# One-core attention and expert kernel: slot table and row order made by one-hot products instead of index scatters, one raw-key buffer, two squares at step 4

## The chip, the cores and the metric

The kernel runs on one core of a Trainium2 chip. A core has five engines with a queue of instructions each: TensorE (PE, matmuls and transposes), VectorE (DVE), ScalarE (ACT), GpSimd (POOL) and SyncE (SP, which here issues most DMAs). Transfers run on 16 DMA engines. An engine takes its instructions in order; one that waits holds back all behind it. The metric is the device time of one execution, in microseconds; the median of the runs counts.

## What is computed

Attention with pooled queries, then routed experts, then a gated product with two more weight matrices:

```python
B, H, S, D = q.shape                                    # 4, 8, 1152, 64
q_pool = q.reshape(B, H, S // 2, 2, D).mean(axis=3)     # 576 rows
scores = np.matmul(q_pool, k.transpose(0, 1, 3, 2)) / np.sqrt(D)
attn = exp(scores - max); attn /= attn.sum(-1) + 1e-9
x = np.matmul(attn, v)                                  # -> (2304, 512)

do_compute = x @ w_skip > 0                             # rows that go to an expert
logits = x[do_compute] @ w_gate                         # 8 experts
e_idx, gate_w = argmax(logits), softmax(logits)[e_idx]
for e in range(8):                                      # w1 (512,1024), w2 (1024,512) of expert e
    y[e_idx == e] = gate_w * (relu(x @ w1[e]) @ w2[e])
out[do_compute] = x + y ; the other rows stay x

a, b = out @ m1, out @ m2                               # (512,1024) each
result = ((a * b) @ w3) @ w_out                         # (1024,1024), (1024,512)
```

m1, m2, w3 and w_out come as 64-bit floats and are brought to 32 bits in the kernel.

## The kernel before

**Attention.** 16 pairs of heads p, four for each of four batches; a pair has nine steps, which a loop runs through as i = 0..143 (p, l = divmod(i, 9)) and a few more to drain. Step i issues, in this order: on PE the nine transposes (L289) of step i−2's probabilities, whose three parts ACT, DVE and ACT copy out of PSUM (L308); on ACT the exponentials (L278) of step i−1; on PE the products with v (L325); on PE the score matmuls (L255) of step i, and on DVE their maximum (L266). POOL prepares keys (L208, L209) and queries (L214 to L222) of later pairs in `prep`, SP moves them. The raw keys `kr` have two buffers. Between the transposes and copies, and at the end of a step, `side` lets two generators go on by a piece:

- `conv_ops` brings the 64-bit weights to 32 bits, chunk by chunk: a load to `ch`, the square L82 (on POOL, 128x512), the scaling and bit operations L96 to L104 (on DVE), a store. The squares of the first two chunks stand together in one piece.
- `route_ops` routes one batch of 576 rows (five groups j of 128 rows) once its attention is done: expert and skip score, one-hot rows, ranks by a triangular matmul (L391, L393; the banks are the `VB` pair), then for each row a place `si` in the table of slots (expert e begins at e·2304) and a place `sp` in the order of all rows. Ten indirect DMAs on POOL (`put`, L417) scatter the row numbers `idt` by these to the DRAM tables `tab` and `perm`. Then five groups of rows x are turned by PE (L448), scaled by DVE (L451) into one of four `xr` buffers, given their gate weight (L454) and stored by SP to `x_d` (L456). The batches 0, 1 and 2 are routed inside the loop, from steps 44, 80 and 116 on.

**Transition.** The last batch is routed after the loop. Between its pieces `fill` issues pieces of `wprime`, the product of w3 and w_out (matmuls L513, b<-CC,WS; blocks RW of w3 are loaded by ACT, L558, split into a high and a low half by ACT, L554, and DVE or POOL, L555 and L556). `emit_meta` computes on DVE the table of expert tiles (first slot and expert of each); only with it does SP issue the loads of W1 (L608) and read the 128 row numbers of a tile from `tab` (`ld_idx`, L587). `ORD` is read from `perm` (L823). POOL gathers rows of `x_d` by them (L592 for tiles, L568 for the final groups), and W1 and W2 are split into halves by ACT, DVE and POOL.

**After it.** 11 expert tiles of 128 rows, then six groups of 384 rows with m1, m2 and the product of wprime, scattered to the output by `ORD`.

The code is issued in the order in which it is written; the engines run it by semaphores.

Of the kernel before, what the change touches and what calls it, by code (L numbers as in the profile page):

```python
# [19 lines left out]
NTT = 5  # L20
# [8 lines left out]
NJ = NTILE + 1  # L29
CW = 512  # L30
# [13 lines left out]
def body(ctx, tc, q, k, v, w9, w1, w2, m1, m2, w3t, wo, cst, mcst, ids, out, dbg=None):  # L44
# [17 lines left out]
    padt = const.tile([128, 145], I32, name="padt")  # L62

    x_d = dram.tile([N, XW], F32, name="x_d")
    tab = dram.tile([SLOTS + 128, 1], I32, name="tab")
    perm = dram.tile([N, 1], I32, name="perm")
# [7 lines left out]
    def conv_ops(erl):  # L74
# [12 lines left out]
        ms = [sq(nxt[0]), sq(nxt[1])]  # L87
        for n, (name, c) in enumerate(conv_q):
# [31 lines left out]
    if True:  # L120
# [7 lines left out]
        KH = [pl[i].tile([128, S], F32R, name=f"kh{i}") for i in range(2)]  # L128
        KL = mid.tile([128, S], F32R, name="kl")
# [9 lines left out]
        def load(p):  # L139
# [4 lines left out]
            rawk[p] = erl.tile([128, S], F32, tag="kr", name="kr", bufs=2)  # L144
# [192 lines left out]
        def route_ops(b, hook=None):  # L337
# [69 lines left out]
            si = keep.tile([128, NTT, 1], I32, tag="si", name="si")  # L407
            DVE.tensor_scalar(si, po, float(PADID), None, op0=ALU.add)
# [3 lines left out]
            sp_ = keep.tile([128, NTT, 1], I32, tag="sp", name="sp")  # L412
            DVE.tensor_tensor(sp_, tp_, pb[:, :, NE:NE + 1], op=ALU.add)
            scat = {id(tab): [], id(perm): []}

            def put(t, ix, j, top):
                m = POOL.indirect_dma_start(  # L417
                    out=t[:, :], out_offset=bass.IndirectOffsetOnAxis(ap=ix[:, j, :], axis=0),
                    in_=idt[:, b, j:j + 1], in_offset=None, bounds_check=top, oob_is_err=False).ins
                for e in scat[id(t)]:  # L420
                    tc.declare_no_dep(m, e, reason="other slots")
                scat[id(t)].append(m)

            if hook:
                for j in range(NTT):
                    put(tab, si, j, SLOTS - 1)
                for j in range(NTT):
                    put(perm, sp_, j, N - 1)
            else:
                for j in range(NTT):  # L430
                    put(tab, si, j, SLOTS - 1)
                    put(perm, sp_, j, N - 1)
                    yield "C"
# [543 lines left out]
```

## Time and profile before

| | us |
|---|---|
| median of 3 runs (1098.1 to 1102.2) | 1099.67 |
| profiled execution, its own time | 1107.73 |
| its span in the trace | 1105.6 |
| PE busy in the span | 1031.4 (93%) |
| DVE busy | 583.6 (53%) |
| ACT busy | 482.3 (44%) |
| POOL busy | 393.7 (36%) |
| attention and routes of batches 0 to 2 | until about 560 |
| last route and wprime | about 560 to 632 |
| expert tiles | 632 to 780 |
| final groups | 780 to 1106 |

A share of busy time is a mean over stretches with different limits. The clock in the windows is the one that PE was granted, as a share of 2.4 GHz. Idle time is put down to the event that came last before the engine went on.

### The profile page before, as it was taken

The numbers are of one execution on the slowest core, as the hardware profiler recorded it, in microseconds if no ns is written. First come the engines' busy times: TensorE is split into PE (matmuls) and PEld (weight loads), VectorE is DVE, ScalarE is ACT, GpSimd is POOL, SyncE is SP. The second block draws the span as 40 slices with busy tenths as digits, with TensorE's granted clock in tenths as the row PEclk, the third lists the DMA queues.
The fourth block names the chain that finished last, engine by engine and source line by source line (L and its number), as shares of the span: only waits on it lengthen the run. The fifth ranks groups of instructions, "written<-read, shape, count | busy, mean of one in ns | idle before, by whom it ended". The sixth has DMA issues, their size and how long they took to land. (4 is left out here: it accounts for less than half of the span.)

```text
span 1105.6 us, 16864 instructions
## 1 busy us (share of the span) xinstructions
PE 1031.4 (93%) x6060; PEld 834.8 (76%) x6060; DVE 583.6 (53%) x883; ACT 482.3 (44%) x903; POOL 393.7 (36%) x411
## 2 busy tenths in 40 slices
PE   5799999999999899899998699998899999999995
PEld 4577776777767677676776488786799898989894
DVE  6588888788876788775633322437531221213120
ACT  4466665666655566565521322434432221212120
POOL 4643524563544435250824623439301010110101
PEclk9899999999999999999999699999899999999998
DMA  9776787587874878527518841506101010100000
GB/s 265 193 229 195 225 234 219 117 192 218 250 223 89 186 212 251 151 66 150 163 39 125 265 168 40 188 24 240 34 10 48 14 44 20 39 33 26 29 1 31
DMA packets 73003, 144.92 MB, mean 131 GB/s; under 512 B 16576, under 2 KB 26304, under 8 KB 72898
## 3 DMA queue, kind: packets, MB, share of 16 engines
q1 hardware_dynamic: 63698, 127.79, 41.7%
q0 software_dynamic: 6080, 14.26, 4.0%
q10 hardware_dynamic: 3120, 1.57, 0.9%
q8 instruction: 53, 0.87, 0.4%
q14 instruction: 52, 0.43, 0.1%
HBM read 86.23 MB, written 22.96 MB: 99 GB/s over the span
## 5 line engine op out<-in xcount | busy, mean ns | idle before, releaser
L266 DVE TENSOR_REDUCE sm<-s 128x1 f32<-128x1152 f32 x144 | 195.3, 1356 | 117.5 <-PE s L255 91.5
L255 PE MATMUL s<-k,q 128*128 128x384 f32 x864 | 204.9, 364 | 29.4 <-DVE pt L308 17.3
L255 PEld LDWEIGHTS s<-k,q 128*128 128x128 f32 x864 | 147.2, 192 | 98.1 <-issue 46.9
L308 ACT COPY pt<-s 128x384 f32<-128x384 f32 x288 | 137.6, 479 | 179.9 <-PE s L289 173.9
L278 ACT ACTIVATE p<-s,sm 128x1152 f32<-128x1152 f32 x144 | 176.3, 1224 | 16.6 <-DVE sm L266 16.1
L325 PE MATMUL vb<-pt,vr 128*64 128x256 f32 (+1 forms) x1152 | 170.7, 418 | 4.3 <-DVE xr L451 2.5
L289 PE MATMUL s<-cs,p 128*128 128x128 f32 x1296 | 169.7, 277 | 4.0 <-ACT p L278 3.6
L289 PEld LDWEIGHTS s<-cs,p 128*128 128x128 f32 x1296 | 151.2, 143 | 14.8 <-ACT p L278 7.5
L887 DVE TENSOR_TENSOR ar<-b,ar 128x384 f32<-128x384 f32 x48 | 26.7, 557 | 189.7 <-PE b L883 189.7
L902 POOL DMA_INDIRECT out_dram<-ar,ord x18 | 17.9, 994 | 271.0 <-ACT ar L901 266.3
L325 PEld LDWEIGHTS vb<-pt,vr 128*64 128x64 f32 x1152 | 70.2, 136 | 56.7 <-issue 22.5
L308 DVE COPY pt<-s 128x384 f32<-128x384 f32 x144 | 78.8, 547 | 2.7 <-PE s L289 1.8
L209 POOL TENSOR_TENSOR kl<-kr,kh 128x384 fp32r<-128x384 f32 x45 | 47.5, 1056 | 77.2 <-DMA k<-kl 66.6
L888 ACT CAST CVh<-ar 128x384 fp32r<-128x384 f32 x48 | 24.6, 513 | 107.7 <-DVE ar L887 107.7
L82 POOL TENSOR_TENSOR cm<-ch 128x512 f32<-128x512 f32 x40 | 42.1, 1057 | 76.1 <-DVE ca L104 47.1
L513 PE MATMUL b<-W1h,CVh 128*128 128x512 f32 x176 | 60.1, 402 | 0.7 <-issue 0.5
L513 PE MATMUL b<-W2h,CVh 128*128 128x512 f32 x176 | 60.7, 404 | 0.2
L513 PE MATMUL b<-WPh,CVh 128*128 128x512 f32 x144 | 57.4, 399 | 0.0
L513 PE MATMUL b<-WPl,CVh 128*128 128x512 f32 x144 | 56.9, 395 | 0.0
L513 PE MATMUL b<-WPh,CVl 128*128 128x512 f32 x144 | 56.8, 394 | 0.0
L901 ACT COPY ar<-b 128x512 f32<-128x512 f32 x18 | 10.6, 587 | 86.2 <-PE b L513 86.2
L208 POOL TENSOR_SCALAR kh<-kr 128x384 fp32r<-128x384 f32 x45 | 26.3, 584 | 57.9 <-PE s L255 52.1
(194 smaller groups left out, 1799.0 us busy)
## 6 DMA issues: line engine op xcount, KB each, us to landing
R<-in_w_dram SPq DMA_DIRECT2D x16, 1024.0 KB, 8.8
vr<-in_v_dram SPq DMA_DIRECT2D x16, 576.0 KB, 4.9
kr<-in_k_dram SPq DMA_DIRECT2D x15, 576.0 KB, 5.3
qr<-in_q_dram SPq DMA_DIRECT2D x15, 576.0 KB
k<-kh SPq DMA_DIRECT2D x30, 288.0 KB, 5.7
k<-kl SPq DMA_DIRECT2D x30, 288.0 KB, 15.3
q<-qnl SPq DMA_DIRECT2D x60, 144.0 KB, 4.2
ch<-in_w3t_dram SPq DMA_DIRECT2D x16, 512.0 KB, 4.8
```

The lines of the kernel that those rows point to most:

```text
L82: POOL.tensor_tensor(m, hf, hf, op=ALU.mult)
L208: POOL.tensor_scalar(KH[i][:, cc], rawk[p][:, cc], 1.0, 0.0, op0=ALU.mult, op1=ALU.add)
L209: POOL.tensor_tensor(KL[:, cc], rawk[p][:, cc], f(KH[i][:, cc]), op=ALU.subtract)
L255: m = PE.matmul(sp[:, c, 0:384], lhsT=lt, rhs=kk[:, 384 * c:384 * c + 384], start=(n == 0), stop=(n == len(seq) - 1))
L266: DVE.tensor_reduce(sm, sp[:, :, 0:384], axis=AX.XY, op=ALU.max, negate=True)
L278: ACT.activation(pt, sp[:, :, 0:384], AF.Exp, bias=sm, scale=1.0, accum_out=SM[b][:, hp, c:c + 1])
L289: m = PE.transpose(tp[:, u * 128:u * 128 + 128], src[:, kt * 128:kt * 128 + 128], ident)
L308: m = (DVE.tensor_copy(o, i_) if eng is DVE else ACT.copy(o, i_)).ins
L325: PE.matmul(acc[64 * h:64 * h + 64, 0:n], lhsT=vr[:, h, kt, :], rhs=pt[:, kt, h, :], start=(kt == 0), stop=(kt == KT - 1))
L513: PE.matmul(o, lhsT=lh[a], rhs=rh[b_], start=(first and n == 0), stop=(last and n == len(order) - 1))
L887: DVE.tensor_tensor(cv, pb[:, 0:GT], av, op=ALU.mult)
L888: ACT.copy(CV[0][:, c], cv)
```

## The change

1. *Index tables without scatters.* `tab`, `perm` and their first filling are gone. A table `slots` (128 x 164: 144 + 2 columns for the slots, 18 for the order) stays in SBUF. For each group j four tensor_scalars make one-hot matrices: place & 127 against a row of 0..127 (twice, 128x128), place >> 7 against 0..145 and 0..17, multiplied by row number + 1. They stand in one of two buffers `ob` and are made on POOL for the batches 0 to 2; in the last route on DVE, in R3's memory, for all five groups. Two matmuls of 146 and 18 columns (L452, or L443 for all groups together) give the group's part of the table, which DVE adds to `slots`. The five groups of a batch each take a "P" piece of `route_ops`: steps 55, 57, 58, 59 and 62 for batch 0 and 36 and 72 later. The five groups of x move by one such place. The last route has one "P" more, so that two more pieces of `wprime` come ahead of what follows it.
2. *Reading.* `ld_idx` copies a column of `slots` from SBUF to SBUF; `ORD` is a view of the last 18 columns, with no load.
3. *Constants.* At i = 2 a matmul and four DVE operations make the row 0..145.
4. *Raw keys.* `kr` has one buffer; the second head of pair 0 is loaded into `kl`.
5. *Squares.* The two first squares have a piece for themselves, called at i = 4; the conversion then goes on from step 6 instead of 8. The steps of the route that only let the conversion go on ("C") are gone.

```diff
-            rawk[p] = erl.tile([128, S], F32, tag="kr", name="kr", bufs=2)
+            rawk[p] = erl.tile([128, S], F32, tag="kr", name="kr", bufs=1)
...
-                rawk[0, h] = erl.tile([128, S], F32, tag="kr", name="kr", bufs=2)
+                rawk[0, h] = f(KL) if h else erl.tile([128, S], F32, tag="kr", name="kr", bufs=1)
...
-            def put(t, ix, j, top):
-                m = POOL.indirect_dma_start(
-                    out=t[:, :], out_offset=bass.IndirectOffsetOnAxis(ap=ix[:, j, :], axis=0),
-                    in_=idt[:, b, j:j + 1], in_offset=None, bounds_check=top, oob_is_err=False).ins
...
-                    put(tab, si, j, SLOTS - 1)
-                    put(perm, sp_, j, N - 1)
-                    yield "C"
...
+            DVE.tensor_scalar(hl[:, 0], si, 127, None, op0=ALU.bitwise_and)
+            DVE.tensor_scalar(hl[:, 1], si, 7, None, op0=ALU.logical_shift_right)
+            hf_ = keep.tile([128, 2, 2, NTT], F32, tag="hf", name="hf", bufs=1)
+            DVE.tensor_copy(hf_, hl)
+            E = DVE if hook else POOL
...
+            def build(j):
+                t = ob[j] = obs[j % len(obs)]
+                for u in range(2):
+                    E.tensor_scalar(t[:, 128 * u:128 * u + 128], iota[:, 0:128], hf_[:, 0, u, j:j + 1], None,
+                                    op0=ALU.is_equal)
+                for u, c0, n in ((0, 256, NSL), (1, 256 + NSL, NCNT)):
+                    E.tensor_scalar(t[:, c0:c0 + n], iota[:, 0:n], hf_[:, 1, u, j:j + 1], idf[:, b, j:j + 1],
+                                    op0=ALU.is_equal, op1=ALU.mult)
...
+            for j in range(len(obs)):
+                build(j)
+            if len(obs) == NTT:
+                yield "P"
+                tp = tbank()
+                for u, c0, n in parts:
+                    for j in range(NTT):
+                        t = ob[j]
+                        PE.matmul(tp[:, c0:c0 + n], lhsT=t[:, 128 * u:128 * u + 128], rhs=t[:, 256 + c0:256 + c0 + n],
+                                  start=(j == 0), stop=(j == NTT - 1))
+                DVE.tensor_tensor(slots, tp[:, 0:NSL + NCNT], slots, op=ALU.add)
             else:
                 for j in range(NTT):
+                    yield "P"
+                    tp = tbank()
+                    t = ob.pop(j)
+                    for u, c0, n in parts:
+                        PE.matmul(tp[:, c0:c0 + n], lhsT=t[:, 128 * u:128 * u + 128], rhs=t[:, 256 + c0:256 + c0 + n],
+                                  start=True, stop=True)
+                    DVE.tensor_tensor(slots, tp[:, 0:NSL + NCNT], slots, op=ALU.add)
+                    if j + len(obs) < NTT:
+                        build(j + len(obs))
             if hook:
-                hook()
+                fr_ = hook[1]
+                DVE.tensor_scalar(fr_, slots, 0.0, float(PADID + 1), op0=ALU.is_equal, op1=ALU.mult)
+                DVE.scalar_tensor_tensor(TAB, slots, -1.0, fr_, op0=ALU.add, op1=ALU.add)
+                hook[0]()
...
-            SP.dma_start(IDX[j % 5], tab[bass.ds(st, 128), :])
+            SP.dma_start(IDX[j % 5], TAB[:, bass.ds(st, 1)])
...
-                        if g == 1 and i > 7:
-                            side("DC")
+                        if g == 1 and i > 5:
+                            side("D")
...
+                if i == 4:
+                    next(conv)
...
-            SP.dma_start(ORD, perm.rearrange("(c p) o -> p (c o)", p=128))
```

How the instructions stand on their engines at three places follows; the line numbers are those of each kernel, so that L82, L208, L214 and L222 of before are L83, L211, L217 and L225 of after.

POOL in the steps 3 to 7, before (`bd` and `qnl` are pair 1's queries, `kh` and `kl` pair 2's keys, `qsum` its queries, `cm` the squares):

```order
L222 TENSOR_SCALAR bd_110<-qnl 64x64 x2
L208 TENSOR_SCALAR kh_111<-kr 128x384
L209 TENSOR_TENSOR kl<-kr,kh_111 128x384
L208 TENSOR_SCALAR kh_111<-kr 128x384
L209 TENSOR_TENSOR kl<-kr,kh_111 128x384
L208 TENSOR_SCALAR kh_111<-kr 128x384
L209 TENSOR_TENSOR kl<-kr,kh_111 128x384
L214 TENSOR_TENSOR qsum<-qr 128x576
L215 TENSOR_SCALAR qsum<-qsum 128x576
L82 TENSOR_TENSOR cm<-ch 128x512 x2
```

The same place after:

```order
L225 TENSOR_SCALAR bd_110<-qnl 64x64 x2
L83 TENSOR_TENSOR cm<-ch 128x512 x2
L211 TENSOR_SCALAR kh_111<-kr 128x384
L212 TENSOR_TENSOR kl<-kr,kh_111 128x384
L211 TENSOR_SCALAR kh_111<-kr 128x384
L212 TENSOR_TENSOR kl<-kr,kh_111 128x384
L211 TENSOR_SCALAR kh_111<-kr 128x384
L212 TENSOR_TENSOR kl<-kr,kh_111 128x384
L83 TENSOR_TENSOR cm<-ch 128x512
L217 TENSOR_TENSOR qsum<-qr 128x576
```

The first two squares moved from behind pair 2's keys to ahead of them, and the third to directly behind them.

PE at the end of step 55 and the beginning of step 56, before (`s` the scores' bank, `vb` the bank of the products with v):

```order
L255 MATMUL s<-k_116,q_101 128x384
L255 MATMUL s<-k_116,q_102 128x384
L255 MATMUL s<-k_116,q_101 128x384
L255 MATMUL s<-k_116,q_102 128x384
L289 MATMUL s<-cs,p 128x128 x9
L325 MATMUL vb_91<-pt_2021,vr 64x256 x4
```

And after (`ob` is a buffer of one-hot matrices):

```order
L258 MATMUL s<-k_118,q_101 128x384
L258 MATMUL s<-k_118,q_102 128x384
L258 MATMUL s<-k_118,q_101 128x384
L258 MATMUL s<-k_118,q_102 128x384
L452 MATMUL vb_91<-ob_113 128x146
L452 MATMUL vb_91<-ob_113 128x18
L292 MATMUL s<-cs,p 128x128 x9
L328 MATMUL vb_91<-pt_2034,vr 64x256 x4
```

The first group's two matmuls stand between the scores of step 55 and the transposes of step 56; POOL builds `ob` where its first scatters stood.

SP in the last route, before (`R` is a half of W1, `ix` a tile's 128 row numbers):

```order
L608 DMA R_5577<-in_w_dram 128x4x512
L456 DMA x_d<-xr_83 128x516
L456 DMA x_d<-xr_84 128x516
L456 DMA x_d<-xr_85 128x516
L456 DMA x_d<-xr_86 128x516
L456 DMA x_d<-xr_83 64x516
L823 DMA ord<-perm 128x18x1
L586 TENSOR_LOAD meta
L586 ISA x2
L587 REGISTER_ALU
L587 DMA ix_120<-tab 128x1
```

And after:

```order
L634 DMA R_5607<-in_w_dram 128x4x512
L482 DMA x_d<-xr_83 128x516
L482 DMA x_d<-xr_84 128x516
L482 DMA x_d<-xr_85 128x516
L482 DMA x_d<-xr_86 128x516
L482 DMA x_d<-xr_83 64x516
L612 TENSOR_LOAD meta
L612 ISA x2
L613 ISA
L613 DMA ix_122<-slots 128x1
```

The load of ORD is gone, and the index column comes from `slots`; the order of W1, the stores and the columns is the same.

## Rows read from the trace of the kernel before

**Rows 1.** Windows: us; busy (count) PE, PEld, DVE, ACT, POOL; clock, DMA share, GB/s.

```profile
60.00:560.00 500.00, 480.13 (x3276) 355.63 (x3275) 385.92 (x544) 310.08 (x586) 227.19 (x244) 1.00 0.69 186
...
604.00:632.00 28.00, 13.45 (x41) 10.19 (x40) 6.43 (x11) 7.18 (x13) 14.77 (x16) 0.70 0.79 233
```

**Rows 2.** PE's waits on DVE's copy: us in total, times, longest.

```profile
PE s L255 <- DVE pt L308: 17.3, 11, 6.3
```

**Rows 3.** PE's timeline, begin of steps 8, 9 and 11: start, us, operation.

```profile
35.91 1.15 PE L289 MATMUL s<-cs,p 128*128 128x128 f32 x9
...
39.39 1.15 PE L289 MATMUL s<-cs,p 128*128 128x128 f32 x9
...
54.58 1.15 PE L289 MATMUL s<-cs,p 128*128 128x128 f32 x9
```

**Rows 4.** Timelines of POOL and DVE around the first squares.

```profile
30.86 0.54 POOL L222 TENSOR_SCALAR bd<-qnl 64x64 fp32r<-64x64 f32 x2
...
43.40 2.03 POOL L82 TENSOR_TENSOR cm<-ch 128x512 f32<-128x512 f32 x2
...
30.76 0.55 DVE L308 COPY pt<-s 128x384 f32<-128x384 f32 x1
...
44.47 1.51 DVE L96 SCALAR_TENSOR_TENSOR cm<-cm,ch 128x512 f32<-128x512 f32 x1 [6.48 <-POOL cm L82]
```

**Rows 5.** PE's timeline: steps 58 and 60, then 94, 96 and 99.

```profile
220.85 1.15 PE L289 MATMUL s<-cs,p 128*128 128x128 f32 x9
...
227.88 1.15 PE L289 MATMUL s<-cs,p 128*128 128x128 f32 x9
...
353.75 1.15 PE L289 MATMUL s<-cs,p 128*128 128x128 f32 x9
...
364.36 1.20 PE L289 MATMUL s<-cs,p 128*128 128x128 f32 x9
...
379.60 2.01 PE L255 MATMUL s<-k,q 128*128 128x384 f32 x6 [2.04 <-DMA q<-qnh]
```

**Rows 6.** DMA queues from 592 to 596 us: packets, MB, share of 16 engines.

```profile
q1 hardware_dynamic: 174, 0.35, 83.3%
q0 software_dynamic: 25, 0.00, 0.5%
```

**Rows 7.** DMA queue of the same kind from 618 to 624 us.

```profile
q1 hardware_dynamic: 761, 1.53, 71.8%
```

**Rows 8.** Timelines around the transition: SP's issues, DVE, ACT, POOL, PE.

```profile
610.37 0.53 SPq L823 DMA_DIRECT2D ord<-perm  x1
612.33 2.77 SPq L587 DMA_DIRECT2D ix<-tab  x3
...
609.01 0.68 DVE L451 TENSOR_TENSOR xr<-vb,r 64x512 f32<-64x512 f32 x1 [12.93 <-DMA x_d<-xr]
...
611.49 1.04 ACT L554 CAST WSh<-RW 128x1024 fp32r<-128x1024 f32 x1 [16.62 <-DMA RW<-w3t]
...
615.56 1.30 POOL L592 DMA_INDIRECT xr<-x_d,ix  x1 [19.51 <-DVE W1l L634]
...
613.07 0.80 PE L513 MATMUL b<-CCh,WSh 128*128 128x512 f32 x1 [9.04 <-ACT WPr L552]
...
632.13 0.50 PE L513 MATMUL b<-W1h,CVh 128*128 128x512 f32 x1 [0.50 <-issue]
```

**Rows 9.** Small operations: timelines of PE and DVE; by line, ns minimum/median/maximum.

```profile
206.75 0.70 PE L393 MATMUL vb<-oh,csr 128*128 128x50 f32 x5
...
213.51 0.17 DVE L413 TENSOR_TENSOR sp<-tp,pb 128x5 int32<-128x5 f32 x1
...
214.32 1.15 PE L289 MATMUL s<-cs,p 128*128 128x128 f32 x9
...
L222 POOL TENSOR_SCALAR bd<-qnl x30: 236/328/1095, 30.9 to 480.0; 64x64 fp32r<-64x64 f32 x30
...
L208 POOL TENSOR_SCALAR kh<-kr x45: 506/512/959, 21.7 to 473.6; 128x384 fp32r<-128x384 f32 x45
```

More of the change, by code (lines that the diff above doesn't have):

```diff
@@ L29 @@
 NJ = NTILE + 1
+NSL = NE * NCNT + 2
 CW = 512
@@ L128, in body @@
         KH = [pl[i].tile([128, S], F32R, name=f"kh{i}") for i in range(2)]
+        OB = [mid.tile([128, 256 + NSL + NCNT], F32R, name=f"ob{i}") for i in range(2)]
         KL = mid.tile([128, S], F32R, name="kl")
@@ L406, in route_ops @@
             DVE.scalar_tensor_tensor(po, cm, -float(PADID), po, op0=ALU.mult, op1=ALU.add)
[L407 to L408 removed]
+            si = keep.tile([128, 2, NTT], I32, tag="si", name="si")
+            DVE.tensor_scalar(si[:, 0].unsqueeze(2), po, float(PADID), None, op0=ALU.add)
             tp_ = keep.tile([128, NTT, 1], F32, tag="tp", name="tp")
@@ L424, in route_ops @@
-            if hook:
-                for j in range(NTT):
-                    put(tab, si, j, SLOTS - 1)
-                for j in range(NTT):
-                    put(perm, sp_, j, N - 1)
+            DVE.tensor_tensor(si[:, 1].unsqueeze(2), tp_, pb[:, :, NE:NE + 1], op=ALU.add)
+            hl = keep.tile([128, 2, 2, NTT], I32, tag="hl", name="hl", bufs=1)
+            DVE.tensor_scalar(hl[:, 0], si, 127, None, op0=ALU.bitwise_and)
+            DVE.tensor_scalar(hl[:, 1], si, 7, None, op0=ALU.logical_shift_right)
@@ L558, in wprime @@
                     ACT.dma_start(RW[fc % 2], wv["w3"][:, :, 128 * (fc + 4):128 * (fc + 4) + 128])
+        TAB = slots.bitcast(I32)
+        ORD = TAB[:, NSL:NSL + NCNT]
         IDX = [keep.tile([128, 1], I32, name=f"ix{i}") for i in range(5)]
         a0, a1 = (AR[i].rearrange("p a c -> p (a c)") for i in range(2))
-        ORD = keep.tile([128, N // 128], I32, name="ord")
         NTG = GT // 128
@@ L774, in body @@
                         DVE.tensor_copy(csr, cs[:, C_U:C_U + 256])
+                    if i == 2:
+                        PE.matmul(VB[1][:, 0:128], lhsT=ones, rhs=tri, start=True, stop=True)
+                        DVE.tensor_copy(iota[:, 0:128], VB[1][:, 0:128])
+                        DVE.tensor_scalar(iota[:, 128:NSL], iota[:, 0:NSL - 128], 128.0, None, op0=ALU.add)
+                        DVE.tensor_scalar(idf, idt, 1.0, None, op0=ALU.add)
                 if l in (8, 0, 1, 3, 4, 5) and rts.get("k") == "P":
@@ L811, in hook @@
                 ld_w(R1, w1, 0, 3)
-            rg = route_ops(NB - 1, hook)
+            r3 = R3.rearrange("p a f -> p (a f)").bitcast(F32R)
+            rg = route_ops(NB - 1, (hook, a0[:, 0:NSL + NCNT]),
+                           [r3[:, 512 * j:512 * j + 256 + NSL + NCNT] for j in range(NTT)])
             pieces = {0: 1, 2: 1, 4: 3, 5: 3}
```

32 lines of the change are left out of this document (13 added, 19 removed).

## The prediction

> **What bounds the kernel now.** The stretches come first. From 60 to 560 us TensorE is busy for 480.13 of 500 us, so the attention is its own bound: what another engine saves there counts only where TensorE stands still, and each instruction that is put on TensorE counts in full. From 604 to 632 us, between attention and expert tiles, it is busy for 13.45 of 28 us, at a mean granted clock of 0.70, while DMA is busy for 0.79 [rows 1]. So three places are left.
>
> *Steps 8 to 11.* The list of TensorE's waits has 17.3 us in 11 waits of the score matmuls on the copy L308 of DVE, one of them 6.3 us long [rows 2]. TensorE's rows show it: steps 8, 9 and 11 begin at 35.91, 39.39 and 54.58, with this wait between the last two [rows 3]. DVE did not come to its copy because it stood at L96, which waited 6.48 us for the first squares; POOL made these only at 43.40, behind the raw-key work of step 6, although its step-5 work had ended at 30.86 + 0.54 = 31.40 [rows 4].
>
> *Steps 94 and 95, right behind a route's index scatters.* These two take 364.36 − 353.75 = 10.61 us; the same two steps of the route before take 227.88 − 220.85 = 7.03. In step 99 the scores wait 2.04 us for a transfer of q [rows 5]. The stall of steps 130 and 131, in the next route, reads alike. DVE's copies, POOL's scatters and the transfers all end late there.
>
> *The transition.* Around the last scatters 174 packets keep 16 engines busy for 83.3% of 4 us: 0.833 · 64 / 174 = 0.306 us for a packet [rows 6]. Later 761 packets take 71.8% of 6 us, or 0.718 · 96 / 761 = 0.091 [rows 7]. Both are blocks of weights and rows. In the chain, the first store of x_d frees its buffer for DVE only at 609.01, after 12.93 us, the fifth store follows, then ORD is read from perm at 610.37, then the index columns, and the first gather runs at 615.56. On the other arm ACT gets w3's last block at 611.49, and TensorE goes on with wprime at 613.07 after 9.04 us of nothing. The first matmul of an expert tile starts at 632.13 [rows 8].
>
> **The change part by part.** The profiled execution took 1107.73 us, 8.06 above the median of the runs; the sum is made against it and brought to the median at the end.
>
> *Squares at step 4.* They follow on POOL at 31.40, where it then idles until the copies of pair 0 are done. At 1.0 each, the first ends at 32.4 and the second at 33.4; DVE has ended its copy of step 6 at 31.3 [rows 4], so about 1 us of wait is left, of which I count 0.7 against TensorE. Steps 9 and 10, 54.58 − 39.39 = 15.19, should take twice the 3.48 between steps 8 and 9 [rows 3]: 6.96. The gain is 8.23 − 0.7 = 7.5 (bounds 6.5 and 8.2). Next late there would be the key work of step 6, which the squares push back by 2 us; POOL waited longer than that for its buffers.
>
> *One raw-key buffer.* Nothing: a pair's raw keys are consumed well before the next load is issued, and SP already waits for KL's stores in front of it. The second head of pair 0 in KL holds POOL's first write of KL until DVE's key work is over, near 16, and POOL comes there at 22.
>
> *No scatters in the attention.* The stalls of the routes of batches 1 and 2 are 2 · (10.61 − 7.03) = 7.2, and 2.04 more at step 99 [rows 5]: 9.2. The route of batch 0 scatters too and shows no stall, so the bounds are 0 and 11; I take it all, as nothing else differs in these steps from those of the other route.
>
> *One-hot products in its place.* For three batches, 15 pairs of matmuls. The nearest matmuls, 128x50, take 0.70 for five, 0.14 each with the last one's way through counted; I take 0.2 a pair: 3.0 (at most 4.2), all of it on TensorE. A build is four tensor_scalars on POOL; the nearest are 0.328 (64x64, from 0.236 to 1.095) and 0.512 (128x384) [rows 9]. So about 0.35 each, 1.4 a build (bounds 0.95 and 4.4). The first build of a batch starts behind DVE's indices, which end at 213.68 now and near 214.2 with the added shift, mask and copy; it ends at 215.6, whereas TensorE is done with step 55 at 214.32 [rows 9]. TensorE stands still for 1.3 to 1.4, and behind the waiting matmul all transposes of step 56: 3 · 1.4 = 4.2 (bounds 2.5 and 13). The other four builds have a step or more each. POOL loses ten scatters at 1.3 in return, DVE gains 0.25 a pair in its own gaps. The iota at step 2 is a matmul and some DVE work: 0.4.
>
> *The last route.* Twenty DVE builds at about 0.15, 3 us, end near 581.7; TensorE comes to the ten matmuls at 579.6 and waits 2.1. The meta table follows some 5 us later than now, so SP issues W1 at about 592 instead of 586.6, with the x_d stores behind it. Against that, no scatter slows the queues: w3's block, W1 and the first store are 2.9 MB, 1400 packets of 2 KB; at 0.091 on 16 engines 8 us, and the store lands near 603, 6 before now. Without the ORD load (610.37 to 612.33, 1.96) the index columns come at 606, the first gather at about 609 against 615.56 [rows 8], three gathers of the final groups at 1.3 behind it, landed near 615.3. On the other arm w3's block lands near 597, so wprime runs through and ends near 613; its last POOL split, which now stands behind the gathers and costs 4.2, comes ahead of them. Then eight transposes and casts: the first expert matmul at 616.5 instead of 632.13, a gain of 15.6 [rows 8]. Bounds: 8, if the gathers come as late as wprime lets them and the clock falls as between 604 and 632 [rows 1]; 19, if the builds' wait hides. The later W1 has cover: its split for the first half needs only ACT and DVE, at 0.6 a chunk.
>
> *Sum.* 7.5 + 9.2 + 15.6 − 3.0 − 4.2 − 0.4 = 24.7, so 1083.0 for the profiled execution and 1075 for the median.
>
> **A rule against this.** The slow packets stand beside scatters of a few bytes [rows 6]; whether these are the cause is what the gain hangs on. The Trainium skill, DMA: Bandwidth & Descriptors, section "SWDGE vs HWDGE vs iDMA", says that each DMA engine has 16 internal queues, that transfers issued by GpSimd and by SP or ACT feed different ones, and that the engine takes turns between them. By that rule a few hundred tiny packets would cost a weight transfer only their own turns, and the sum would be that of the first rival, 1097; the packet time, over three times as long, speaks against it.
>
> **The rivals.**
> *The scatters are not what slows the transfers.* Then the stalls of steps 94, 95 and 99 stay, and of the transition only the ORD load and the last split go, less the builds: about 3. The sum is 7.5 + 0 + 3 − 7.6 = 2.9: 1097. For it: batch 0 scatters without a stall. Against it: 0.306 and 0.091 [rows 6, 7]. Chance 0.08.
>
> *TensorE waits for the builds (slower than before).* Builds of 6.5 us make it wait 6.4 in step 55, none in 57, 1.9 in 58 and 3.2 in 59, 11.5 a batch or 34.5: with the other terms, 7.5 + 9.2 + 15.6 − 3.0 − 0.4 − 34.5 = −5.6, the median is 1105; from there on it is slower. Even four of L222's longest, 4.4, would make it 1084 [rows 9]. The spread of L222, 0.236 to 1.095, is what speaks for it. Chance 0.03. The Trainium skill, GPSIMD Engine Reference, section "8. Key points", has a reason for such a spread: GpSimd shares its way into SBUF with VectorE.
>
> *The transition gives half back.* Either the gathers start on the old schedule because SP's in-order queue now has W1 later ahead of the stores, or TensorE idles and starts the tiles at half clock, as the granted clock of 0.70 shows it does now [rows 1]. T3 would be 4 to 10: 1081 to 1087, up to 1094 if one of the other gains is half its size too. Chance 0.20.
>
> *More than that.* The transfers of the whole routes run faster and the pt stalls of [rows 2] shrink beyond the two places: 1056 to 1066. Chance 0.09. And should the squares not move ahead on POOL, the first term goes: 1083, inside the forecast.
>
> **How the numbers follow.** Forecast, 1066 to 1084: 0.60. Half given back, 1084 to 1094: 0.20. Scatters not to blame: 0.08. Slow builds: 0.03. Better: 0.09. The range 1065 to 1090 leaves out the 0.08 and 0.03, most of the 0.09, and part of the 0.20. Within 0.5%, what a measurement of this kernel can tell, is 1094.2 to 1105.2: 0.08 for the first rival. Faster 0.89, slower 0.03.
>
> **What would show it.** Right: POOL's first squares before 33 and no wait over 1 us of TensorE in steps 8 to 10; steps 94 and 95 in 7 us plus the one-hot matmuls; waits of 1 to 2 us before the first one-hot matmul of a batch; packets near 0.09 us at 595; the first expert matmul near 607 (616.5 less 7.5 and 9.2, plus 7.6). Wrong: packets of 0.3 us without scatters, one-hot builds over 2 us, or a gap of several us at half clock ahead of the first tile.

## The result, and the profile after

The changed kernel takes 1089.54 us in the median of 4 runs (1086.69 to 1089.68), the kernel before 1100.93 (1098.1 to 1104.25) beside it: a ratio of 0.989, with an interval from 0.986 to 0.992. On a second chip, in a run of the same file, it was 0.988 (0.985 to 0.992). It is faster, as forecast, and 1089.54 lies at the upper end of the range of 1065 to 1090; but the gain is 11.4 us where 24.7 were forecast.

The two profiled executions lie 18.1 us apart (1107.73 and 1089.66). The forecast for the profiled execution was 1083.0, so the mechanisms account for 6.7 us of the error of 14.5, and the other 7.9 are the step from the profile to the median. First where these 18 us are. The windows of the profile after, with the columns of [rows 1] (us; busy time and count of PE, PEld, DVE, ACT, POOL; clock; DMA share; GB/s):

```profile
60.00:560.00 500.00, 484.82 (x3302) 358.28 (x3300) 378.34 (x557) 306.14 (x582) 232.51 (x271) 0.99 0.65 182
560.00:604.00 44.00, 40.99 (x185) 33.38 (x184) 25.15 (x92) 8.35 (x12) 8.42 (x5) 0.92 0.36 111
604.00:632.00 28.00, 23.12 (x102) 17.97 (x101) 14.89 (x17) 11.46 (x21) 20.12 (x18) 0.88 0.94 339
```

From 604 to 632 us TensorE is now busy for 23.12 us instead of 13.45, and the DMA engines move 339 GB/s instead of 233. But the stretch before it, which in the trace before had no gap and full clock,

```profile
560.00:604.00 44.00, 44.00 (x219) 34.68 (x215) 17.41 (x64) 8.12 (x13) 16.88 (x14) 1.00 0.47 74
```

has lost 3 us of TensorE's time and has a granted clock of 0.92. The marks of both traces divide the 17.7 us by which the spans differ (1105.6 and 1087.9):

| | before | after | gain | forecast |
|---|---|---|---|---|
| begin of the last transposes (attention) | 553.96 | 546.19 | 7.8 | 9.1 |
| from there to the first expert matmul | 78.17 | 71.01 | 7.2 | 15.6 |
| expert tiles, to the first matmul of the final groups | 148.71 | 151.00 | −2.3 | 0 |
| final groups, to the last matmul | 311.64 | 310.91 | 0.7 | 0 |
| from the last matmul to the end of the span | 13.12 | 8.79 | 4.3 | 0 |

TensorE's waits after (us in total, times, longest), against [rows 2]:

```profile
PE s L258 <- DVE pt L311: 6.5, 9, 2.3
PE vb L452 <- POOL ob L431: 5.9, 3, 2.0
...
PE vb L602 <- DMA ar<-x_d,slots: 3.9, 3, 3.4
PE vb L443 <- DVE R L431: 3.0, 4, 1.6
```

The 17.3 us on DVE's copies have become 6.5. The other three lines are new: two wait for the one-hot matrices that the change brought (L452 in the attention, L443 in the last route), and one for the rows of the first final group (L602). Steps 8 to 11 and 91 to 93 on PE (start, us, operation, in brackets idle time before and what ended it), and the first squares on POOL:

```profile
36.72 1.20 PE L292 MATMUL s<-cs,p 128*128 128x128 f32 x9
40.23 1.15 PE L292 MATMUL s<-cs,p 128*128 128x128 f32 x9
...
47.13 1.14 PE L292 MATMUL s<-cs,p 128*128 128x128 f32 x9
...
338.73 1.14 PE L292 MATMUL s<-cs,p 128*128 128x128 f32 x9
...
344.35 0.69 PE L452 MATMUL vb<-ob 128*128 128x146 f32 x2 [1.98 <-POOL ob L431]
344.90 1.20 PE L292 MATMUL s<-cs,p 128*128 128x128 f32 x9
346.03 1.83 PE L328 MATMUL vb<-pt,vr 128*64 128x256 f32 x8
347.79 2.14 PE L258 MATMUL s<-k,q 128*128 128x384 f32 x6
349.77 1.14 PE L292 MATMUL s<-cs,p 128*128 128x128 f32 x9
...
31.00 2.04 POOL L83 TENSOR_TENSOR cm<-ch 128x512 f32<-128x512 f32 x2
```

Steps 9 and 10 take 47.13 − 40.23 = 6.90 us instead of 15.19 [rows 3], with the squares at 31.00 instead of 43.40 [rows 4]. Steps 91 and 92 take 11.04 us (338.73 to 349.77). The trace before has 6.75 for them, from the first of these rows to the second:

```profile
343.73 1.15 PE L289 MATMUL s<-cs,p 128*128 128x128 f32 x9
...
350.48 1.15 PE L289 MATMUL s<-cs,p 128*128 128x128 f32 x9
```

The difference is 1.98 of waiting for POOL's first build, and then a step whose products with v take 1.83 instead of 1.08 and whose scores take 2.14 instead of 1.34. In that stretch the granted clock was 0.65, a mean of time at 1.2 and time at 2.4 GHz:

```profile
344.90:349.80 4.90, 4.90 (x25) 3.63 (x26) 2.22 (x4) 2.17 (x4) 4.90 (x8) 0.65 0.27 64
353.10:360.50 7.40, 7.40 (x56) 6.01 (x54) 5.31 (x8) 4.34 (x8) 7.08 (x10) 1.00 0.53 124
```

The second of these windows holds steps 94 and 95: 7.40 us with their one-hot products, against 10.61 [rows 5].

The transition after, against [rows 8]:

```profile
571.92 0.31 PE L443 MATMUL vb<-R 128*128 128x146 f32 x1
...
575.54 0.49 PE L443 MATMUL vb<-R 128*128 128x146 f32 x1 [1.60 <-DVE R L431]
...
577.70 0.77 PE L538 MATMUL b<-CCh,WSh 128*128 128x512 f32 x1
...
613.30 1.11 PE L602 MATMUL vb<-cs,ar 128*128 128x128 f32 x4 [3.38 <-DMA ar<-x_d,slots]
...
617.20 0.79 PE L538 MATMUL b<-W1h,CVh 128*128 128x512 f32 x1
...
573.67 1.55 DVE L428 TENSOR_SCALAR R<-iota,hf 128x128 fp32r<-128x128 f32 x2
...
573.78 1.36 POOL L581 TENSOR_TENSOR WSl<-RW,WSh 128x512 fp32r<-128x512 f32 x1 [4.38 <-ACT WSh L579]
...
585.50 1.00 SPq L634 DMA_DIRECT2D R<-in_w_dram  x2
...
597.68 1.05 ACT L579 CAST WSh<-RW 128x1024 fp32r<-128x1024 f32 x1 [4.86 <-DMA RW<-w3t]
...
600.66 0.47 SPq L482 DMA_DIRECT2D x_d<-xr  x1
...
604.49 1.23 POOL L618 DMA_INDIRECT xr<-x_d,ix  x1 [3.88 <-DMA ix<-slots]
```

The 9.04 us wait and the wait for POOL's last split are gone. In their place stand 5.8 us at the ten products (571.92 to 577.70; 3.0 of them are waiting, in four waits for the builds), a stretch at half clock behind them (0.50 from 577.70 to 581.70), and 3.4 us for the rows of the first final group. One of DVE's pairs of builds took 1.55 us instead of 0.47 while POOL had its split beside it.

### The profile page after: what moved, and what is told of

Read it like the earlier page. It is cut to its first block, busy times and chain, and to the rows that moved or that the text cites. A ratio compares the mean times of both kernels' runs of the same rounds, so it can differ in the third digit from the quotient of the medians.

```text
span 1087.9 us, 16931 instructions
## 1 busy us (share of the span) xinstructions
PE 1034.7 (95%) x6101; PEld 836.4 (77%) x6101; DVE 594.7 (55%) x935; ACT 481.6 (44%) x903; POOL 394.8 (36%) x431
## 5 line engine op out<-in xcount | busy, mean ns | idle before, releaser
L328 PE MATMUL vb<-pt,vr 128*64 128x256 f32 (+1 forms) x1152 | 173.5, 422 | 4.6 <-DVE xr L477 2.1
L292 PEld LDWEIGHTS s<-cs,p 128*128 128x128 f32 x1296 | 147.8, 142 | 11.9 <-ACT p L281 6.0
L935 POOL DMA_INDIRECT out_dram<-ar,slots x18 | 18.0, 1001 | 271.3 <-ACT ar L934 266.7
L311 DVE COPY pt<-s 128x384 f32<-128x384 f32 x144 | 78.9, 548 | 3.0 <-PE s L292 3.0
L83 POOL TENSOR_TENSOR cm<-ch 128x512 f32<-128x512 f32 x40 | 43.2, 1084 | 68.0 <-DVE ca L106 46.1
L934 ACT COPY ar<-b 128x512 f32<-128x512 f32 x18 | 10.5, 586 | 86.2 <-PE b L538 86.2
L211 POOL TENSOR_SCALAR kh<-kr 128x384 fp32r<-128x384 f32 x45 | 27.5, 611 | 55.6 <-PE s L258 52.3
```

The costliest lines, as they stand in the source:

```text
L83: POOL.tensor_tensor(m, hf, hf, op=ALU.mult)
L211: POOL.tensor_scalar(KH[i][:, cc], rawk[p][:, cc], 1.0, 0.0, op0=ALU.mult, op1=ALU.add)
L292: m = PE.transpose(tp[:, u * 128:u * 128 + 128], src[:, kt * 128:kt * 128 + 128], ident)
L311: m = (DVE.tensor_copy(o, i_) if eng is DVE else ACT.copy(o, i_)).ins
L328: PE.matmul(acc[64 * h:64 * h + 64, 0:n], lhsT=vr[:, h, kt, :], rhs=pt[:, kt, h, :], start=(kt == 0), stop=(kt == KT - 1))
```

## The experiments

Two theories. **A**: the gains are those of the forecast's mechanisms (squares, scatters), and what is missing is what the one-hot products cost, in the attention with the clock and in the transition with the order of the transfers. **B**, the rival: some of the stalls in the first profile belonged to that execution only, or the scatters are not what causes them.

**The kernel before, profiled again** (no edit).

> The kernel before, unchanged, profiled a second time. Theory A (the stalls belong to the kernel): steps 9 and 10 again take about 15 us, steps 94 and 95 about 10.6, the wait for q in step 99 about 2, the first expert matmul comes near 632 us and the last 10 us behind the last ACT copy stay; the span is within 2 us of 1105.6. Theory B (part of what the first profile shows is particular to that execution, which lay 7 us above the median): the stall of steps 9 and 10 stays, but some of the others are gone, and the span is near 1098.

Span 1107.2 us. Steps 9 and 10 took 15.8 us, steps 94 and 95 10.62, the first expert matmul came at 634.41. The waits:

```profile
PE s L255 <- DVE pt L308: 16.4, 9, 6.4
PE b L513 <- ACT WPr L552: 10.8, 1, 10.8
```

Theory A: the stalls return in their places. The exception is step 99: it took 4.4 us here and 7.1 in the first profile, so the long wait for q there belonged to the first profiled execution.

**The squares alone**, in the kernel before:

```diff
         ms = [sq(nxt[0]), sq(nxt[1])]
+        yield
...
-                        if g == 1 and i > 7:
+                        if g == 1 and i > 5:
...
+                if i == 4:
+                    next(conv)
```

> The kernel before with only the squares moved (own piece, called at step 4, conversion from step 6). Theory A: steps 9 and 10 take 7 us instead of 15.2, nothing else changes, so the time falls by 7.5 us, to a ratio of 0.993. Theory B (the time comes back later, because DVE or the transfers catch up at some other step): less than 3 us, a ratio over 0.997.

Ratio 0.993 (0.990 to 0.996), 8 us of this chip's 1107.38. Step 12 began at 50.61 instead of 57.84. The term is right, and it stays to the end. But something else did change: with all scatters in place, steps 94 and 95 took 7.01 us here (they begin at 349.75 and step 96 at 356.76), and steps 130 and 131 took 13.81 instead of 10.59. POOL's rows tell these apart. Here squares of the conversion stood between the scatters of the second route, four scatters, a square, four, a square, two:

```profile
347.06 0.97 POOL L418 DMA_INDIRECT perm<-idt,sp  x1 [0.30 <-issue]
348.10 1.04 POOL L82 TENSOR_TENSOR cm<-ch 128x512 f32<-128x512 f32 x1
349.29 1.28 POOL L418 DMA_INDIRECT tab<-idt,si  x1 [0.15 <-issue]
```

In the third route all ten ran in a row. The same holds in the two profiles of the kernel before: the route of batch 0, with a square after every four scatters, has no stall, and the routes of batches 1 and 2, with eight and ten in a row, have 3.6 to 4.2 us each. No run spaced the scatters and changed nothing else, so this goes together but is not shown as the cause.

**No scatters in the attention**, in the kernel before:

```diff
-                    put(tab, si, j, SLOTS - 1)
-                    put(perm, sp_, j, N - 1)
                     yield "C"
...
+            SP.dma_start(perm.rearrange("(p n) o -> p (n o)", p=128), padt[:, 0:18])
```

> The kernel before without the 30 scatters of batches 0 to 2 (left out: their slots stay empty, so their rows go through no expert and are not written; the last batch's ten scatters stay). Theory A (the scatters cause the stalls behind them): steps 94 and 95, and 130 and 131, take 7.0 us instead of 10.6, the wait in step 99 is gone, the attention ends 9 us earlier. The transition keeps its slow packets. Theory B (the scatters are not to blame): these steps stay as they are, the attention ends at 554 us within 2.

Ratio 0.986 (0.980 to 0.993). The begins of steps 95 and 96 on PE:

```profile
357.49 1.15 PE L289 MATMUL s<-cs,p 128*128 128x128 f32 x9
...
360.74 1.14 PE L289 MATMUL s<-cs,p 128*128 128x128 f32 x9
```

Step 94 began at 353.71, so that 94 and 95 took 7.03 us. Steps 130 and 131 took 7.03 too. From step 55 to the end of the attention this kernel gained 11.6 us on the first profile; the forecast had 9.2 (bounds 0 and 11). So without scatters there is no stall in these steps. Of the whole time less was gained in this profile (span 1096.7): the transition, which keeps its ten scatters, took 84.2 us in this execution instead of 78.2. The end of the span is shorter here too; of that below.

**The scatters back**, into tables that nobody reads, in the changed kernel:

```diff
...
+            if hook:
+                for j in range(NTT):
+                    put(tab, 0, j, SLOTS - 1)
+                for j in range(NTT):
+                    put(perm, 1, j, N - 1)
...
+                if not hook:
+                    put(tab, 0, j, SLOTS - 1)
+                    put(perm, 1, j, N - 1)
                 yield "P"
```

> The changed kernel plus the 40 scatters of the kernel before, into tables that nobody reads: ten for each of batches 0 to 2, two with each group of rows that is turned and stored, and ten ahead of the builds in the last route. Theory A: stalls of 3 to 4 us come back behind the scatters of at least two routes, and packets of the last route take about 0.3 us again, so that w3's block, W1 and the x_d stores land 5 to 10 us later; in all 10 to 20 us slower than the changed kernel, a ratio to the kernel before near 1.0 to 1.01. Theory B: within 3 us of the changed kernel, a ratio near 0.99.

Ratio 1.010 (1.004 to 1.017), 1.022 times the changed kernel's 0.989, some 24 us; the medians, 1119.76 and 1089.54, lie 30 us apart and the spans 29. That is more than the 10 to 20 expected. Both effects came back. In the attention, which ended at 564.03 instead of 546.19, TensorE waited at steps 72 and 108 for transfers of q; these waits ended 11 and 26 us behind the last scatter of the route. In the last route, right behind the scatters, the packets were slow again. The waits:

```profile
PE s L260 <- DMA q<-qnh: 6.3, 1, 6.3
...
PE s L260 <- DMA q<-qnl: 4.1, 1, 4.1
```

The DMA queue (packets, MB, share of 16 engines) of this kernel from 608 to 612 us, where only SP's queue ran,

```profile
q1 hardware_dynamic: 118, 0.24, 69.6%
```

and of the changed kernel from 586 to 590 us, where W1's load begins:

```profile
q1 hardware_dynamic: 506, 1.02, 79.3%
```

0.696 · 64 / 118 = 0.38 us for a packet with scatters, 0.793 · 64 / 506 = 0.10 without, as [rows 6] against [rows 7]. From the end of the attention to the first expert matmul it was 78.9 us, against 71.0 without the scatters and 78.2 before. So the scatters cost the transition 7.9 us, all that the change gained there. In all profiles of kernels with this order of the last route it was 78.2 to 84.2 us with the ten scatters (five profiles) and 70.0 to 71.5 without (three). By the Trainium skill, DMA: Bandwidth & Descriptors, section "SWDGE vs HWDGE vs iDMA", an engine takes turns between its queues; in the window of 608 to 612 no GpSimd packet ran at all, and SP's packets were slow all the same. Why they stay slow for some us behind the scatters, no run here shows.

**The first one-hot product one piece later**, in the changed kernel:

```diff
             for j in range(len(obs)):
                 build(j)
+            if not hook:
+                yield "D"
             if len(obs) == NTT:
```

> The changed kernel with the first one-hot product of batches 0 to 2 one or two steps behind its builds (a pause between them), the later pieces of the route moved along. Theory A (the wait for the first build costs 2 us and, in two of three routes, a step at the lower clock besides, 11 us in all over the 0.2 a pair): steps 55 and 56 take 6.8 us instead of 9.5, steps 91 and 92, 127 and 128 6.8 instead of 11; the attention ends 10 us earlier, a ratio to the kernel before near 0.980. Theory B (PE waits elsewhere for the same builds or for DVE): less than 4 us, a ratio over 0.985.

Ratio 0.974 (0.970 to 0.979): 1079.22 us, 10 less than the changed kernel, with the attention ended at 536.61 instead of 546.19. The window up to step 91, with TensorE busy throughout at full clock, and the begins of steps 91 and 93:

```profile
328.00:339.00 11.00, 11.00 (x77) 8.21 (x76) 6.84 (x17) 6.70 (x14) 3.05 (x5) 1.00 0.54 207
```

```profile
336.21 1.15 PE L292 MATMUL s<-cs,p 128*128 128x128 f32 x9
...
342.96 1.14 PE L292 MATMUL s<-cs,p 128*128 128x128 f32 x9
```

Steps 91 and 92 take 6.75 us, as in the kernel before. Two lines of code bring another 10 us in the attention; the wait and the clock behind it were the price of the change there.

**The rows of the first final group later** (gathers behind the split of W1, transposes behind the tiles):

```diff
             gather(0)
-            ld_x(0, XG)
             gather(1)
...
             split(W1, R1, 4)
+            ld_x(0, XG)
...
             xpose(0)
-            for t in range(NTG):
-                x2t(X2a, t, XG[t])
...
                 split_cols(c0, c1)
+                if c0 == 0:
+                    for t in range(NTG):
+                        x2t(X2a, t, XG[t])
```

> The changed kernel with the second tile's gather ahead of the three gathers of the first final group, these behind the split of W1, and their transposes behind the expert tiles. Theory A (in the transition TensorE waits for these three gathers, which share the DMA engines with the weights): the 3.4 us wait goes, the first expert matmul stands about 2 us behind the last product of wprime instead of 8, some 5 us earlier; 4 to 5 us of it stay to the end, a ratio near 0.985. Theory B (then the W1 split of POOL or the W2 load is late): the first tile takes longer, 1 us or nothing is left.

Ratio 0.984 (0.979 to 0.988); the span is 1088.9, against 1087.9 of the changed kernel. The first expert matmul did come 64.2 us behind the end of the attention instead of 71.0, but the transposes, now behind the tiles, waited there for the last tile's scatter:

```profile
PE vb L602 <- DMA x_d<-xr,ix: 3.7, 1, 3.7
```

Of 6.8 us, 4.7 were given back between the first expert matmul and the final groups (155.7 us instead of 151.0), and the attention of this execution had ended 2.2 later. The expectation of A on the start was right; the span did not fall. The ratio would fit A, but its interval overlaps that of the changed kernel on its two chips.

**Meta table and W1 first**, twelve pieces of wprime ahead of the ten products:

```diff
+            if hook:
+                hook[0]()
+                yield "F"
             for j in range(len(obs)):
                 build(j)
+                if hook and j in (1, 3):
+                    yield "F"
...
-                hook[0]()
...
+                else:
+                    fill(3 if kind == "F" else 0)
```

> The changed kernel with the meta table and W1's load ahead of the one-hot builds in the last route, and twelve pieces of wprime instead of three issued between them and the ten matmuls. Theory A (TensorE's 5.8 us at the one-hot products and the lower clock behind it are the builds' length, and W1's load ahead of w3's block and the stores makes the first tile late): no wait there, W1 issued at about 579 instead of 585.5, the first gather 3 us earlier, the first expert matmul 4 to 6 us earlier, a ratio near 0.984. Theory B (the start of the tiles hangs on the x_d stores and the gathers, whose time does not move): wprime ends 8 us earlier, TensorE waits as much longer for the rows, 1 us or nothing is left.

Ratio 0.985 (0.981 to 0.989), span 1089.5. TensorE no longer waited at the products, and wprime ended 56.3 us behind the attention instead of 62.9. But then it stood for the rows:

```profile
PE b L672 <- DMA xr<-x_d,ix: 7.4, 1, 7.4
...
PE vb L606 <- DMA ar<-x_d,slots: 4.0, 1, 4.0
```

B: the pieces of wprime had pushed the turning of the rows back, and the first expert matmul came 72.8 us behind the attention instead of 71.0. The three edits together:

> The three edits together: the first one-hot product later, the first final group's rows behind the tiles' start, meta table and W1 first. Theory A: the gains add, 10 + 8 to 12 us on the changed kernel, a ratio near 0.971. Theory B: what one edit gives another takes back, a ratio over 0.98.

Ratio 0.976 (0.972 to 0.981), between the two thresholds, and no better than the later one-hot product alone on the same chip (1081.31 and 1079.22 us). The first expert matmul came 5.2 us earlier behind the attention than there, and the tiles took 7.2 longer, so what B says of the edits holds.

**The changed kernel again**, on another chip:

> The changed kernel, unchanged, timed again on another chip with more runs of the kernel before. Theory A (the gain is that of the two profiles, 18 us, and the 11 us of the first medians came out of few runs): a ratio of 0.983 to 0.986. Theory B (the profiles overstate it): 0.988 to 0.991.

Ratio 0.988 (0.985 to 0.992), span 1087.9. B: the difference of medians is near 13 us (1.2% of 1103.83), that of the profiles near 18 to 20.

**Rows first**: four groups turned and stored ahead of the builds, W1 loaded behind the index columns.

```diff
+            if hook:
+                yield from gates()
+                yield from rows(range(4))
             for j in range(len(obs)):
                 build(j)
+                if hook and j in (1, 3):
+                    yield "F"
...
+            ld_w(R1, w1, 0, 3)
             gather(0)
...
```

> The changed kernel with another order in the last route: the first four groups of rows are turned and stored ahead of the one-hot builds, the fifth behind them, then the products and the meta table; W1 is loaded behind the index columns; four pieces of wprime stand between the builds. Theory A (the start of the tiles is set by the chain x_d store, index column, gather, W1's split, and TensorE's time in wprime can cover it): no wait of TensorE at the ten products, the first gather near 595 instead of 604.5, the first expert matmul 9 to 13 us earlier and 8 to 12 us less in all, a ratio near 0.975. Theory B (W1, now later, takes the place of the rows): the tiles start within 3 us of where they did, a ratio over 0.982.

Ratio 0.986 (0.982 to 0.990), and with the later one-hot product:

> The same order in the last route, and the first one-hot product of batches 0 to 2 behind a pause as in the run with that edit alone. Theory A: the gains add, 10 to 12 us beyond the run with the later one-hot product alone, a ratio near 0.965. Theory B: within 3 us of that run, a ratio near 0.974.

0.978 (0.973 to 0.982). B in both: the first expert matmul came 70.2 and 70.1 us behind the attention; rows and wprime were earlier, and now W1 was late. ACT's first split of it in the first of the two kernels:

```profile
607.30 2.18 ACT L675 CAST W1h<-R 128x512 fp32r<-128x512 f32 x4 [8.83 <-DMA R<-in_w_dram]
...
612.75 0.62 ACT L675 CAST W1h<-R 128x512 fp32r<-128x512 f32 x1 [3.28 <-DMA R<-in_w_dram]
```

**Rows, then meta table and W1, then the builds**, with the later one-hot product:

```diff
                 yield from rows(range(4))
+                yield "F"
+                hook[0]()
+                yield "F"
...
```

> The changed kernel with the later first one-hot product and another last route: four groups of rows stored first, then the meta table and W1's load, then the builds, each with pieces of wprime between, the fifth group and the ten products last. Theory A (wprime, the rows and W1 are three chains of nearly one length, so that each edit alone leaves the start of the tiles to the next one; with all three earlier the start moves): no wait of TensorE over 2 us between 560 us and the tiles, W1 landed before 590, the first gather before 590, the first expert matmul within 4 us of wprime's end, 9 to 12 us earlier than with the later one-hot product alone (599 instead of 608); a ratio near 0.966. Theory B (the gain is given back in the tiles, which then wait for the next weights): the tiles start earlier, but the last one ends where it did, a ratio of 0.973 or more.

Ratio 0.975 (0.973 to 0.978), 1074.57 us; span 1071.5, 4.5 less than with the later one-hot product alone. The first expert matmul stands at 602.72, 66.7 us behind the attention (71.5 there). Between wprime (last product 592.27) and the tiles TensorE waits only for the three row groups:

```profile
596.14 1.09 PE L621 MATMUL vb<-cs,ar 128*128 128x128 f32 x4 [3.05 <-DMA ar<-x_d,slots]
597.96 1.12 PE L621 MATMUL vb<-cs,ar 128*128 128x128 f32 x4 [0.73 <-DMA ar<-x_d,slots]
601.57 1.12 PE L621 MATMUL vb<-cs,ar 128*128 128x128 f32 x4 [2.49 <-DVE X2l L624]
```

The start moved when all three chains moved, by half of what A expected (5.4 us of 9 to 12), and the tiles gave 0.4 of it back. The ratio, 0.975, is B's and no better than the 0.974 of the later one-hot product alone, which was timed on another chip; so the 4.5 us rest on two profiles and on medians from two chips (1074.57 and 1079.22).

**The same, with these three transposes in the first three tiles**:

```diff
             ymm(2, 4)
+            if j < NTG:
+                x2t(X2a, j, XG[j])
             ymm(4, 8)
```

> The last version (rows, meta table and W1 first, later one-hot product) with the gathers of the first final group behind the gathers of the first two tiles and the split of W1, and the transposes of its three row groups in the first three expert tiles, one each (this needs at least three tiles, as here). Theory A (what is left between wprime's end and the first tile is the wait for these rows and for DVE's part of their transposes, 8 us): the first expert matmul stands 1.5 to 3 us behind the last product of wprime instead of 10.5, and at least 4 of these 8 us stay to the end: a ratio near 0.970. Theory B (the first tile then waits for POOL's split of W1 and W2's load): less than 2 us stays, a ratio of 0.974 or more.

Ratio 0.973 (0.970 to 0.976), 1073.43 us, span 1071.1. The first expert matmul came at 596.69, 60.4 us behind the attention, which is earlier than the forecast's 62.5; but the first tile waited 3.3 and 2.5 us for ACT and DVE, and the tiles had the transposes in them: they took 155.4 us instead of 149.1. The turning of the last tile came at 739.18, against 738.85. The spans are 0.4 us apart, so less than 2 us stayed, as B has it; the ratio lies between the thresholds of both.

## Why the prediction was right or wrong, point by point

Two steps of the forecast failed: the term of the transition, which followed one order of arrival and missed what came late next, and the step from the profile to the median. The term of the first one-hot product was mis-sized, and other errors covered that. The cause itself, the scatters and the squares, was right.

- *Squares*: right. 15.19 us became 6.90, and step 7 grew by 0.7, as counted: 7.47 at step 12, 7.5 forecast. The run with the squares alone confirms it in the time.
- *Scatters in the attention*: right in cause. 9.1 us are gone in the two pairs of steps and in step 99 (9.2 forecast), and from step 55 on 11.6 without the scatters and without anything in their place. But 2.7 of the 9.1 are step 99, which the second profile of the kernel before did not have either; that share is luck of the profile shown. The rival that the scatters are not to blame fell twice: taken away, the stalls went; put back, stalls and slow packets returned. Its argument, that batch 0 scatters without a stall, has an answer in POOL's order: there a square stood after every four scatters.
- *First one-hot product*: the term of 4.2 us was mis-sized. The trace shows 2.0 us of waiting each, not 1.4, since a build takes 2.5 us (1.19 for two 128x128, 1.28 for the other two) against 1.4 estimated. And behind two of the three waits the next step ran at a granted clock of 0.65, which the sum did not have. Steps 55 and 56, 91 and 92, 127 and 128 together lost 2.73 + 4.29 + 4.27 = 11.3 us where the sum had 4.8 with their products. The later pairs cost 0.15 to 0.19 each, as counted. The later product gives 9.6 back.
- *The attention as a whole*: 7.8 against 9.1 is close by luck. The products cost 6.5 us more than counted; some 4 us came from steps for which the forecast had no term (64, 116 and 139 are 1.6, 1.5 and 1.2 us shorter).
- *Transition*: the step that failed most, 7.2 instead of 15.6. The cause, scatters that slow the transfers, is right: with scatters 78.9, without 71.0. What was wrong is what would be late next. The builds took 5.4 us instead of 3, one of them slowed beside POOL's split; TensorE was held at the ten products for 5.8 us, 3.0 of it waiting where 2.1 had been counted and the rest the products themselves, for which the sum had nothing, and then lost some 2 at half clock. So w3's block was loaded behind W1 (586.03 and 585.50), not ahead of it, and landed at 597.68 instead of 589 on this time scale, on which the forecast's times lie 7.8 us earlier; DVE's split of it, in front of the fifth group, held the last store back to 600.66. The first gather ran at 604.49 instead of 601, wprime ended at 609.5 instead of 605, and the rows of the first final group landed 4 us behind that, near 613 instead of 607.5. Rows, W1 and wprime end within a few us of each other. Meta table and W1 first, or rows first, left the start of the tiles within 2 us of where it was; the later rows moved it by 6.8, and 4.7 came back behind it.
- *Outside the sum*: the end of the span is 4.3 us shorter, which the forecast did not have at all. The tiles are 2.3 longer, 2.1 of it in the first two: the first begins at half clock (0.50 until 619.3), and in the second TensorE waits 0.9 for DVE.
- *From profile to median*: the forecast took 8.06 us off, as if every execution of the changed kernel would lie as far below its profile. Its profile lies at its median (1089.66 and 1089.54), and so do those of the changed kernel with the later product and with the scatters back (1077.82 and 1079.22, 1118.87 and 1119.76). The profiles of the kernel before lay 7 and 2 us above their medians, whose runs spread over 1097.8 to 1117.1. Of the 7 us, 2.7 are step 99, in which the second profile was short; why that kernel spreads more stays open. Taking a ratio of the profile, 1083.0 / 1107.73, to the median would have made 1075 as well, so no scaling would have helped: the profile shown was an execution above all four runs beside it, and the forecast worked out what it would save.
- *The rivals and signs*: "half given back" (0.20, 1084 to 1094) is what came, by its second part: TensorE idle ahead of the tiles, and their start at half clock. "TensorE waits for the builds" was the right place, at 2.5 us a build far from the 6.5 from which it decides. Of the signs of being wrong, builds over 2 us and a gap ahead of the first tile at half clock both came; packets of 0.3 us without scatters did not.

## What to carry to other kernels

Where a stall ends, follow all chains that meet there, not the last one: here three of them (a product, rows through memory, weights) ended close together, and three edits to one or two of them brought no gain that these runs can tell. A short wait of TensorE in a loop without slack is worth more than its length, because the step behind it may run at the lower clock; a pause of one step between a build on another engine and the product that takes it cost two lines and gave 10 us. Indirect DMAs of a few bytes were dear in three places in this kernel: behind them packets of another queue took 0.31 and 0.38 us instead of 0.09 and 0.10, TensorE stalled for 3.6 us and more behind eight or ten in a row, and each lengthened the end of the span by 0.1 us. And read two profiles of the same kernel before a sum is made from one: a wait in only one of them is no term.

## What the runs showed of the hardware that was not expected

The time between the last instruction and the end of the span goes with the number of indirect DMAs. The last scatter of the output ends, and the span ends:

| kernel | index scatters | end of the last scatter of the output | span | difference |
|---|---|---|---|---|
| before | 40 | 1094.79 | 1105.6 | 10.8 |
| before, again | 40 | 1096.43 | 1107.2 | 10.8 |
| squares alone | 40 | 1085.44 | 1096.2 | 10.8 |
| changed, scatters back | 40 | 1106.56 | 1117.1 | 10.5 |
| no scatters in the attention | 10 | 1089.21 | 1096.7 | 7.5 |
| changed | 0 | 1081.42 | 1087.9 | 6.5 |

That is 0.1 us for each, behind the last instruction that is counted as work. The kernel without scatters in the attention differs from the kernel before by 30 of them, and the one with scatters back from the changed kernel by 40, so it is these that count. Most of it is GpSimd's last DRAIN instruction, which takes 8.24 us with 40 scatters, 5.79 with 10 and 4.97 with none. The last rows, of the changed kernel and of the one without scatters in the attention:

```profile
1080.44 0.98 POOL L935 DMA_INDIRECT out_dram<-ar,slots  x1 [4.66 <-ACTq L942]
```

```profile
1088.24 0.97 POOL L901 DMA_INDIRECT out_dram<-ar,ord  x1 [4.67 <-ACTq L908]
```

And a wait of 1.98 us in the middle of a stretch at full clock was enough, in two of three places, for the granted clock to fall to its lower level for some us behind it; behind the third, of 1.99 us in step 55, it stayed at 1.00 (204.30 to 213.80). It is not the place that decides: in the other profile of the changed kernel the clock fell behind the wait of step 55 (1.98 us) and not behind that of step 91 (1.96 us):

```profile
210.20:217.00 6.80, 6.75 (x25) 5.07 (x26) 1.76 (x3) 2.17 (x4) 6.44 (x10) 0.50 0.00 0
346.00:353.00 7.00, 5.38 (x40) 4.19 (x42) 4.60 (x7) 3.08 (x6) 7.00 (x12) 1.00 0.12 41
```

Of the 18 such waits in six profiles with this attention, 16 were followed by a step at the lower clock. What tells them apart, no run shows.
